# Router logits of a retention-and-experts kernel: row-block sums kept in PSUM on two column quarters, and one weight piece loaded earlier

## The chip, the cores and the metric

One core of one Trainium2 chip runs the whole program. The metric is the device time of one execution in microseconds, measured over several runs. TensorE (PE in the views, its weight loads PEld) does matrix products from SBUF into PSUM, VectorE (DVE) and ScalarE (ACT) do elementwise work, GpSimd (POOL) does elementwise work and indirect DMAs, and SyncE (SP) issues most plain DMAs, one after the other in program order.

## The reference, cut to what matters

```python
# q, k, v: (4, 8, 768, 64); x = retention(q, k, v) as (3072, 512); 8 experts, F = 1024
xn = x / (np.linalg.norm(x, axis=-1, keepdims=True) + 1e-06)
en = expert_emb / (np.linalg.norm(expert_emb, axis=-1, keepdims=True) + 1e-06)
logits = xn @ en.T / tau
expert_idx = np.argmax(logits, axis=1)
...
gate_w = probs[np.arange(N), expert_idx]      # probs = softmax(logits)
for e in range(E):
    mask = expert_idx == e
    h = np.maximum(x[mask] @ w1[e], 0.0)
    out[mask] = gate_w[mask, None] * (h @ w2[e])
```

## The kernel before, in words

The program has two halves. The first is the retention: 12 steps `m` of the loop over `NM`, each 256 tokens with all 8 heads. A step computes scores (L398), masks them on VectorE (L419), adds the products with the running state (`inter`, L466) and with the values (`intra`, L466), updates the state (`state`, L433), and turns the next step's keys (L367) and queries (L385). ScalarE copies the result into `yTs[m]`, a tile with the 512 features on partitions in `KT` = 4 row blocks of 128 and the 256 tokens along the free axis.

The router works on a step's result one step later. `logits_products` multiplies each of the 4 row blocks of `yTs[m]` (128 features x 256 tokens, fp32) with the scaled expert embedding `enT[:, j]` (128 features x 32 columns, 8 of them real). Row block j writes its own quarter of the PSUM bank's partitions (32j to 32j+31), so the four products go to four column quarters of the array, and none of them adds to another. `logits_rows` transposes the bank in 32x32 blocks on VectorE into `parts` (L523). A token's logits are then still in four parts, on four groups of 32 partitions. `sums` (L533) adds them at the end of each group of steps (`GROUPS`): four small TensorE products with a 0/1 matrix, one for each quarter of the tokens, into a free corner of a PSUM bank. `choose` (L547 to L556) takes the maximum and the first expert that reaches it, `add_counts`, `count` and `ranks` turn that into a slot number, and `place` writes the token's row to the table `tbl` by an indirect DMA from GpSimd. At step 3 the logits of steps 0, 1 and 2 are made in one go.

The second half is the experts. The 64 weight pieces (512 KB each, tile `raw`) come through `load_piece` in 4 buffers; ScalarE and VectorE split each into a high and a low part (`whi` L239, `wlo` L243), and TensorE runs three products for each weight block (L265 first layer, L1117 and L1163 second layer). The first expert starts early: as soon as the first token blocks are placed, `early_slots` reads their table rows (L637), `early_gather` fetches the tokens (`xge`, L628), TensorE turns them (L647), and `products` fills TensorE while VectorE and GpSimd finish the routing of the last steps. SyncE's order there is `early_slots(0)`, the rows of step 8 to memory (`rows`, L502), `early_slots(1)`, `early_slots(2)`, then, behind the last early gather (`gathered`), the first expert's fourth piece (four DMAs, L211), two pieces of its second layer (L220), and the rows of steps 9 and 10. `rows_turn(11)` (L495) reuses the buffer that the rows of step 9 are written from.

Tiles `hh`, `hl` (hidden layer) and `xh`, `xl` (tokens) are laid out with a row pitch taken from `PITCH[e]`.

The order on every engine is the order in which the program is written, since the kernel schedules by hand.

Of the kernel before, what the change touches and what calls it, by code (L numbers as in the profile page):

```python
# [11 lines left out]
F32 = mybir.dt.float32  # L12
F32R = mybir.dt.float32r
# [28 lines left out]
CAP = max(CAPS)  # L42
NXC = -(-CAP // Q)
CAPW = NXC * Q
PITCH = [CAP if c % P == 0 else c if e == NE - 2 else CAPW for e, c in enumerate(CAPS)]
OV = 352
EARLY = 280
TURNED = [c % P > 0 and e < NE - 1 for e, c in enumerate(CAPS)]
# [61 lines left out]
def retention_moe(ctx: ExitStack, tc: tile.TileContext, q, k, v, emb, tau, w1, w2, const, const16, out):  # L110
# [10 lines left out]
    def C(name):  # L121
        lo, hi = _AT[name]
        return cst1[:, lo:hi] if hi <= _C1 else cst2[:, lo - _C1:hi - _C1]
# [255 lines left out]
    def transpose_q(m, s, copy=nc.scalar.copy):  # L379

        if m not in qTs:
            qTs[m] = ap_.tile([P, NQ, 2, KT, Q], F32, name="qT")
        ps = pt_()
        for g in range(NQ):
            nc.tensor.transpose(ps[:, g * P:(g + 1) * P], qs_r[:, m % 3, 4 * s + g], ident)  # L385
        return copy(out=qTs[m].rearrange("p g u j (t s) -> p (g u) j t s", s=2)[..., s],
                    in_=ps.rearrange("p (g t j) -> p g j t", g=2 * NQ, j=KT))
# [124 lines left out]
    def logits_products(m, ps=None):  # L512
        ps = pt_() if ps is None else ps
        for j in range(KT):
            nc.tensor.matmul(ps[j * Q:(j + 1) * Q, :T2], enT[:, j, :], yTs[m][:, j, :], start=True, stop=True,  # L515
                             skip_group_check=True)
        return ps

    def logits_rows(m, ps):
        g = group_of[m]  # L520
        if g not in parts:
            parts[g] = ap_.tile([P, max(map(len, GROUPS)), 2, NQ, Q], F32, name="parts")
        nc.vector.transpose(out=parts[g][:, m - GROUPS[g][0]].rearrange("p u g e -> p (u g) e"),  # L523
                            in_=ps[:, :T2].rearrange("p (g b) -> p g b", b=Q))

    def span(g):
        return slice(2 * GROUPS[g][0], 2 * GROUPS[g][-1] + 2)
# [1 line left out]
    def sums(g, ps=None, fresh=False, room=None):  # L529
        nm = len(GROUPS[g])  # L530
        ps = pt_() if ps is None else ps
        for i in range(NQ):
            nc.tensor.matmul(ps[i * Q:(i + 1) * Q, :2 * nm * NE], C("quarters"),  # L533
                             parts[g][:, :nm, :, i, :NE].rearrange("p m u e -> p (m u) e"), start=not fresh, stop=True,
                             skip_group_check=True)
        at = room if fresh else ps[:, 64:]
        return [a[:, :2 * nm * NE].rearrange("p (n e) -> p n e", e=NE) for a in (ps, at)] + [at[:, 48:48 + NE]]

    chosen = []

    def choose(g, zs):
        z, w, _ = zs
        r = span(g)
        nb = r.stop - r.start
        bc = lambda t: t.unsqueeze(2).broadcast_to([P, nb, NE])
        m = ap_.tile([P, nb], F32, name="m", bufs=1)
        nc.vector.tensor_reduce(out=m, in_=z, axis=AX.X, op=ALU.max)  # L547
        yield
        nc.vector.tensor_tensor(out=z, in0=z, in1=bc(m), op=ALU.subtract)
        yield  # L550
        nc.vector.scalar_tensor_tensor(out=w, in0=z, scalar=0.0,
                                       in1=C("e16").unsqueeze(1).broadcast_to([P, nb, NE]), op0=ALU.is_lt, op1=ALU.add)
        yield
        nc.vector.tensor_reduce(out=wmn[:, r], in_=w, axis=AX.X, op=ALU.min)
        yield
        chosen.append(nc.vector.tensor_tensor(out=oh[:, r], in0=w, in1=bc(wmn[:, r]), op=ALU.is_equal))  # L556
        yield
# [77 lines left out]
    def early_slots(j):  # L635
        n = EROWS[j][1]
        sealed.append(nc.sync.dma_start(out=tb[:n, 0, j], in_=tbl[j * P:j * P + n, :2 + NE]))  # L637
# [173 lines left out]
    for m in range(NM):  # L811
# [12 lines left out]
                i = o[0]  # L824
        n = 2 if m < 7 else 3 if m < 9 else 4
        if m == NM - 2:
            early_slots(1)
            held, ready = ready, []
        if m == 0:
# [21 lines left out]
        if m == 0:  # L851
            state(0)
            state_copy(0)
            state_sums(0)
            next(emb_steps)
            intra(0, 0)
            intra(0, 1)
            transpose_k(1, 0)
            i = transpose_k(1, 1)
            after(load_v(2), i)  # L860
            inter(0)
            transpose_q(1, 0)
            i = transpose_q(1, 1)
            for j in (*load_q(3), load_k(3), load_v(3)):
                after(j, i)
            state(1)
            state_copy(1)
            state_sums(1)
        else:
            inter(m)  # L870
            if nxt:
                i = state(m + 1)
                if 6 < m < NM - 3:
                    for x, (f, s) in enumerate(scales):
                        after(f(m + 2, s), first)
                        if x < n:
                            place_one(i)
                if m == NM - 3:
                    after(scale_k(m + 2, 0), spread)
                    for _ in range(3):  # L880
                        place_one(i)
                    scale_k(m + 2, 1)
                    scale_q(m + 2, 0)
                    place_one(i)
                if m == NM - 2:
                    place(held)
                    after(placed[-len(held)], i)
                    early_slots(2)
                    early_gather(0)
                    early_gather(1)  # L890
                    gathered = early_gather(2)
                    for j, n in EROWS:
                        tokens(n, 0, slice(j, j + 1))
                    load_piece(gathered)
                state_copy(m + 1)
                if m + 3 < NM:
                    after(load_k(m + 3), i)
            if m == 2:
                after(nc.sync.dma_start(
                    out=tbl.rearrange("(e s) c -> e (s c)", e=NE)[:, :FILL * SW].rearrange("e (p x) -> e p x", p=P // NE),  # L900
                    in_=none), i)
            for i in () if m < 3 else (0, 1, 2) if m == 3 else (m - 1,):
                logits_rows(i, logits_products(i))
            if m == NM - 5:
                pad(0, spare(0, 3), True)
            if m == NM - 3:
                pad(1, spare(1, 3, 2 * NE), True)
            if m == NM - 2:
                pad(2, bank("pst1"))
            if nxt:  # L910
                state_sums(m + 1)
                if m == NM - 2:
                    lows[0]()
                transpose_k(m + 1, 0)
                transpose_q(m + 1, 0)
                i = transpose_q(m + 1, 1)
                if m + 3 < NM:
                    after(load_v(m + 3), i)
                transpose_k(m + 1, 1)
                if done is not None:  # L920
                    z = sums(done, spare(0, done % 3), True, spare(0, 3))
                    run_all(choose(done, z))
                    run_all(add_counts(done, z))
                if m == NM - 2:
                    lows[1]()
                if m == NM - 2:
                    load_piece(gathered)
                    load_piece(gathered)
                rows(m - 1, gathered if m == NM - 2 else None)
                intra(m, 0)  # L930
                intra(m, 1)
            else:
                intra(m, 0)
                take(m, 0)
                rows_turn(m - 1, (0,))
                z = sums(done)
                run_all(choose(done, z))
                run_all(add_counts(done, z))
                rows_turn(m - 1, (1,))
                rows(m - 1, x=xs_[m - 1])  # L940
                intra(m, 1)
# [146 lines left out]

    xts = {}

    def columns(name, k, e):
        t = hp.tile([P, k, CAPW], F32R, name=name)
        return t.rearrange("p k c -> p (k c)")[:, :k * PITCH[e]].rearrange("p (k c) -> p k c", k=k)

    def x_turn(e, kt):
        if kt == 0:
            xTs[e] = (columns("xh", KT, e), columns("xl", KT, e))
        xt = xts[e, kt] = mp.tile([P, NXC, Q], F32, name="xt", bufs=2)
        n = blocks_of(e)
        nc.vector.transpose(out=xt[:, :n], in_=xgs[e][:, :n, kt * Q:(kt + 1) * Q])  # L1100
        nc.scalar.copy(out=xTs[e][0][:, kt, :CAPS[e]], in_=xt.rearrange("p n b -> p (n b)")[:, :CAPS[e]])
# [175 lines left out]
    for e in range(1, NE):  # L1277
        nxt = e + 1 < NE
        c = CAPS[e]
        cols = slice(0, c)  # L1280
        hh, hl = columns("hh", FT, e), columns("hl", FT, e)
        gsteps = iter(())
        last = None
        for ft in range(FT):
# [166 lines left out]
```

## Time and profile before

| what | value |
|---|---|
| median of 3 runs | 396.85 us (396.44 to 399.21) |
| the profiled execution | 396.12 us |
| its span on the engines | 394.3 us |
| TensorE matmul busy | 384.3 us, 97% of the span |
| VectorE, ScalarE, GpSimd busy | 252.6, 214.6, 154.8 us |
| granted TensorE clock | 1.0 |

The profiled execution is 0.73 us below the median. The span begins with the first instruction; the rest of the execution's time lies around it. Two of the three runs lie close together and the third is 2.4 us above them.

### The profile page before, as it was taken

The page shows a single profiled execution, that of the slowest core. Times are in us where ns is not written, and L with a number is a line of the kernel's source. Part 1 is how long each engine was busy: PE and PEld are TensorE (multiplying, and loading weights), DVE is VectorE, ACT ScalarE, POOL GpSimd, SP SyncE. Part 2 cuts the span into 40 slices and gives each one's busy share as a digit, 9 for nine tenths or more (in the row PEclk, how much of TensorE's full clock was granted, in tenths as well). Part 3 has the DMA queues.
Part 4 walks back from the last instruction along what each step waited for, and adds up shares of the span by engine and source line. Part 5 has one row for each costly group of instructions (what it writes and reads, how often), then busy time and mean ns, then how long its engine had stood idle before and what let it go on. Part 6 is the DMA issues. An engine that isn't in the chain of part 4 may idle for free.

```text
span 394.3 us, 9699 instructions
## 1 busy us (share of the span) xinstructions
PE 384.3 (97%) x3714; PEld 359.4 (91%) x3714; DVE 252.6 (64%) x536; ACT 214.6 (54%) x383; POOL 154.8 (39%) x177
## 2 busy tenths in 40 slices
PE   7999999988999999999999999999999999999995
PEld 3899888877879898999999999999889999999985
DVE  5496876977988648853871874667357756476500
ACT  3585566655876175526553843935675534573411
POOL 2856397585844614203802510530282131121032
PEclk9999999999999999999999999999999999999999
DMA  7898999689469787976778796886979676675121
GB/s 237 260 305 256 268 267 281 180 240 262 98 197 288 237 249 217 298 183 225 251 244 215 257 333 184 256 282 204 264 259 347 191 230 227 169 240 158 30 107 56
DMA packets 91029, 89.20 MB, mean 226 GB/s; under 512 B 10796, under 2 KB 69548, under 8 KB 90972
## 3 DMA queue, kind: packets, MB, share of 16 engines
q1 hardware_dynamic: 85916, 75.39, 64.1%
q0 software_dynamic: 4880, 13.03, 9.2%
q8 instruction: 31, 0.51, 0.6%
q14 instruction: 26, 0.21, 0.2%
q10 hardware_dynamic: 176, 0.07, 0.1%
HBM read 65.00 MB, written 18.79 MB: 212 GB/s over the span
## 4 chain that ended last, share of the span: by engine, by line
PE 77%; DMA 13%; DVE 4%; issue 2%; SPq 1%; POOL 1%; POOLq 0%; ACT 0%; DVEq 0%
DMA out_dram<-og,si 10%; PE b L265 10%; PE pst L1117 9%; PE py L466 9%; PE py L265 8%; PE py L1117 7%; PE pst L265 6%; PE b L398 6%; PE b L1117 4%; PE pst L433 3%; PE pst L1163 3%; PE b L367 3%; PE b L385 2%; PE b L515 2%; PE pst L1203 2%
## 5 line engine op out<-in xcount | busy, mean ns | idle before, releaser
L243 DVE TENSOR_TENSOR wlo<-raw,whi 128x1024 fp32r<-128x1024 f32 x64 | 77.6, 1217 | 15.9 <-ACT whi L239 12.9
L1144 POOL DMA_INDIRECT out_dram<-og,si x26 | 27.0, 1039 | 115.0 <-ACT og L1134 65.2
L239 ACT CAST whi<-raw 128x1024 fp32r<-128x1024 f32 x64 | 66.1, 1044 | 1.3 <-DMA raw<-in_moe_w_dram 1.2
L628 POOL DMA_INDIRECT xr<-xd,gi x24 | 29.3, 1220 | 29.5 <-ACT sq L297 14.9
L265 PE MATMUL b<-xh,whi 128*128 128x360 f32 (+5 forms) x104 | 34.3, 334 | 0.0
L265 PE MATMUL b<-xl,whi 128*128 128x360 f32 (+5 forms) x104 | 34.1, 332 | 0.0
L265 PE MATMUL b<-xh,wlo 128*128 128x360 f32 (+5 forms) x104 | 34.0, 332 | 0.0
L419 DVE TENSOR_TENSOR pm<-b,mask 128x512 f32<-128x512 f32 x48 | 29.8, 683 | 4.8 <-PE b L398 4.5
L1100 DVE STREAM_TRANSPOSE xt<-xg 128x384 f32<-128x384 f32 (+1 forms) x28 | 15.6, 578 | 25.4 <-DMA xg<-xs 25.3
L270 ACT ACTIVATE hh<-b 128x360 fp32r<-128x360 f32 (+5 forms) x26 | 12.6, 484 | 34.9 <-PE b L265 34.9
L356 POOL TENSOR_TENSOR hh<-whi,cst 128x512 f32<-128x512 f32 x22 | 23.1, 1068 | 19.5 <-DVE pm L419 14.3
L599 POOL DMA_INDIRECT tbl<-zt,sloti x24 | 25.4, 1060 | 12.6 <-DVE sloti L590 3.5
L1117 PE MATMUL pst<-hh,wlo 128*128 128x360 f32 (+4 forms) x88 | 29.4, 334 | 0.8 <-DVE wlo L243 0.8
L1117 PE MATMUL pst<-hl,whi 128*128 128x360 f32 (+4 forms) x88 | 29.4, 334 | 0.0
L1117 PE MATMUL pst<-hh,whi 128*128 128x360 f32 (+4 forms) x88 | 29.3, 332 | 0.0
L265 PE MATMUL py<-xl,whi 128*128 128x384 f32 (+5 forms) x84 | 27.7, 334 | 0.0
L265 PE MATMUL py<-xh,whi 128*128 128x384 f32 (+5 forms) x84 | 27.5, 333 | 0.0
L265 PE MATMUL py<-xh,wlo 128*128 128x384 f32 (+5 forms) x84 | 27.2, 330 | 0.0
L361 POOL TENSOR_TENSOR hl<-wlo,cst 128x512 f32<-128x512 f32 x22 | 22.8, 1052 | 10.0 <-DMA wlo<-in_k_dram 8.3
L466 PE MATMUL py<-pm,vs 128*64 128x128 f32 x384 | 24.4, 277 | 1.0 <-issue 1.0
L398 PE MATMUL b<-qT,kT 64*128 64x128 f32 x384 | 24.7, 278 | 0.0
L466 PEld LDWEIGHTS py<-pm,vs 128*64 128x64 f32 x384 | 21.0, 137 | 3.0 <-issue 1.7
(237 smaller groups left out, 1026.0 us busy)
## 6 DMA issues: line engine op xcount, KB each, us to landing
raw<-in_moe_w_dram SPq DMA_DIRECT2D x60, 512.0 KB, 4.7
whi<-in_q_dram SPq DMA_DIRECT2D x24, 256.0 KB, 4.0
xd<-x SPq DMA_DIRECT2D x48, 128.0 KB, 6.3
wlo<-in_k_dram SPq DMA_DIRECT2D x11, 512.0 KB, 6.1
xs<-xr SPq DMA_DIRECT2D x6, 768.0 KB
og<-yt SPq DMA_DIRECT2D x72, 48.0 KB, 3.1
whi<-in_v_dram SPq DMA_DIRECT2D x6, 512.0 KB
wlo<-in_v_dram SPq DMA_DIRECT2D x6, 512.0 KB
```

The lines of the kernel that those rows point to most:

```text
L239: nc.scalar.copy(out=views[1], in_=views[0])
L243: nc.vector.tensor_tensor(out=views[2], in0=views[0], in1=views[1].bitcast(F32), op=ALU.subtract)
L265: nc.tensor.matmul(acc[:, :w], a, x[:, kt, cols], start=(n == 0), stop=(n == len(todo) - 1))
L356: return eng.tensor_tensor(out=qs_r[:, m % 3, :, a], in0=qin[m % 3][:, a], in1=w, op=ALU.mult)
L361: return eng.tensor_tensor(out=ks_r[:, m % 3, s, h], in0=kin[m % 3][:, h, s], in1=w[:, h], op=ALU.mult)
L398: nc.tensor.matmul(psc[a][:, j], kTs[m][a * D:(a + 1) * D, j, u].rearrange("p s c -> p (s c)"), q_cols(m, a, j, u), start=True, stop=True, ...
L419: o.append(nc.vector.tensor_tensor(out=pm, in0=psc[a], in1=w, op=ALU.mult))
L466: nc.tensor.matmul(pys[m][u][o * D:(o + 1) * D, j], lhsT, rhs, start=first, stop=True, skip_group_check=True)
L599: i = nc.gpsimd.indirect_dma_start(out=tbl[:, :], out_offset=bass.IndirectOffsetOnAxis(ap=sloti[:, n:n + 1], axis=0), in_=zt[:, n], in_off ...
L628: return nc.gpsimd.indirect_dma_start(out=xr[:n, j, :], out_offset=None, in_=xd[:rows_, :], in_offset=bass.IndirectOffsetOnAxis(ap=gi[:n, ...
L1117: nc.tensor.matmul(acc[:, :c], a[:, f], x[:, kt, :c], start=(n == 0), stop=(n == 3 * FT - 1))
L1144: i = nc.gpsimd.indirect_dma_start(out=out[:, :] if h is None else out.rearrange("t (h x) -> (t h) x", h=2), out_offset=bass.IndirectOffse ...
```

## The change

Five edits:

1. `logits_products` makes 8 products of 128 columns in place of 4 of 256. The tokens of a step are taken in two sets of columns (`i` = 0, 1), each set goes to one quarter of the partitions (0 to 31, 32 to 63), and the four row blocks add up there in PSUM.
2. `logits_rows` then transposes 64 partitions x 64 twice in place of 128 x 256, straight into the complete logits, and the four products of `sums` are gone. `choose` reads the logits from `parts` in SBUF and keeps the maximum in PSUM.
3. At step 3 the logits of steps 1 and 2 move between the turns of the next step's keys and queries.
4. The fourth raw piece is loaded on SyncE ahead of `early_slots(1)` and waits for no gather.
5. `hh` and `hl` have the pitch `CAPW` = 416 for all experts, and the tokens of expert 6 have it too (360 before).

```diff
-PITCH = [CAP if c % P == 0 else c if e == NE - 2 else CAPW for e, c in enumerate(CAPS)]
+PITCH = [CAP if c % P == 0 else CAPW for c in CAPS]
...
         for j in range(KT):
-            nc.tensor.matmul(ps[j * Q:(j + 1) * Q, :T2], enT[:, j, :], yTs[m][:, j, :], start=True, stop=True,
-                             skip_group_check=True)
+            y = yTs[m][:, j].rearrange("p (u g b) -> p g u b", u=2, b=Q)
+            for i in range(2):
+                nc.tensor.matmul(ps[i * Q:(i + 1) * Q, :P].rearrange("p (h u b) -> p h u b", h=2, b=Q), enT[:, j, :], y[:, i::2],
+                                 start=(j == 0), stop=(j == KT - 1), skip_group_check=True)
...
-        nc.vector.transpose(out=parts[g][:, m - GROUPS[g][0]].rearrange("p u g e -> p (u g) e"),
-                            in_=ps[:, :T2].rearrange("p (g b) -> p g b", b=Q))
+        for h in range(2):
+            nc.vector.transpose(out=parts[g][2 * h * Q:2 * (h + 1) * Q, m - GROUPS[g][0]],
+                                in_=ps[:2 * Q, 2 * h * Q:2 * (h + 1) * Q].rearrange("p (u b) -> p u b", b=Q))
...
-        for i in range(NQ):
-            nc.tensor.matmul(ps[i * Q:(i + 1) * Q, :2 * nm * NE], C("quarters"),
-                             parts[g][:, :nm, :, i, :NE].rearrange("p m u e -> p (m u) e"), start=not fresh, stop=True,
-                             skip_group_check=True)
...
-        nc.vector.tensor_reduce(out=m, in_=z, axis=AX.X, op=ALU.max)
+        s = parts[g][:, :nb // 2, :, :NE].rearrange("p m u e -> p (m u) e")
+        nc.vector.tensor_reduce(out=m, in_=s, axis=AX.X, op=ALU.max)
...
         if m == NM - 2:
+            load_piece()
             early_slots(1)
...
                         tokens(n, 0, slice(j, j + 1))
-                    load_piece(gathered)
...
-            for i in () if m < 3 else (0, 1, 2) if m == 3 else (m - 1,):
+            if m > 2:
+                i = 0 if m == 3 else m - 1
                 logits_rows(i, logits_products(i))
...
+                if m == 3:
+                    logits_rows(1, logits_products(1))
                 i = transpose_q(m + 1, 1)
...
                 transpose_k(m + 1, 1)
+                if m == 3:
+                    logits_rows(2, logits_products(2))
...
-        hh, hl = columns("hh", FT, e), columns("hl", FT, e)
+        hh = hp.tile([P, FT, CAPW], F32R, name="hh")
+        hl = hp.tile([P, FT, CAPW], F32R, name="hl")
```

TensorE's order at step 3, from the first logits product to the values' products of `intra`, before:

```order
L515 MATMUL b_777<-yT,enT 32x256 x4
L515 MATMUL b_784<-yT,enT 32x256 x4
L515 MATMUL b_790<-yT,enT 32x256 x4
L367 MATMUL b_800<-ident,hl 128x128 x4
L385 MATMUL b_808<-ident,hh 128x128 x4
L385 MATMUL b_814<-ident,hh 128x128 x4
L367 MATMUL b_821<-ident,hl 128x128 x4
L533 MATMUL pst_591<-parts,cst_61 32x48 x4
L466 MATMUL py_698<-pm_710,vs 64x128
```

The same place after the change:

```order
L517 MATMUL b_777<-yT,enT 32x128 x8
L367 MATMUL b_793<-ident,hl 128x128 x4
L385 MATMUL b_801<-ident,hh 128x128 x4
L517 MATMUL b_807<-yT,enT 32x128 x8
L385 MATMUL b_818<-ident,hh 128x128 x4
L367 MATMUL b_825<-ident,hl 128x128 x4
L517 MATMUL b_831<-yT,enT 32x128 x8
L466 MATMUL py_698<-pm_710,vs 64x128
```

Here 24 logits products of 128 columns stand where 12 of 256 stood, in three places instead of one, and the sums product of the group (L533) is gone; the order around it is unchanged.

SyncE's order from the loads of the first three pieces to the rows of steps 9 and 10 (`tb` is the table read of `early_slots`, `xd` the rows in memory), as one piece of the difference:

```order
 L211 DMA raw<-in_moe_w_dram 32x2x512 x4
-L637 DMA tb<-tbl 128x10
-L502 DMA xd<-x 256x1x128 x4
-L637 DMA tb<-tbl 128x10
-L637 DMA tb<-tbl 24x10
+L636 DMA tb<-tbl 128x10
+L502 DMA xd<-x 256x1x128 x4
 L211 DMA raw<-in_moe_w_dram 32x2x512 x4
+L636 DMA tb<-tbl 128x10
+L636 DMA tb<-tbl 24x10
 L220 DMA raw<-in_moe_w_dram 128x2x512 x2
 L502 DMA xd<-x 256x1x128 x8
```

The second L211 row, the fourth piece, stood behind all three table reads and now stands ahead of the second and the third.

## Rows read from the trace of the kernel before

**Rows 1.** The page, part 1: busy time, share of the span, instructions.

```profile
PE 384.3 (97%) x3714; PEld 359.4 (91%) x3714; DVE 252.6 (64%) x536; ACT 214.6 (54%) x383; POOL 154.8 (39%) x177
```

**Rows 2.** Waits of TensorE, whole span: total us, times, longest us.

```profile
PE pst L433 <- issue: 1.2, 1, 1.2
PE py L466 <- issue: 1.0, 1, 1.0
PE pst L1117 <- DVE wlo L243: 0.8, 2, 0.4
```

**Rows 3.** Chain that ended last, by time: start us, us, what.

```profile
38.71 1.43 PE b L515 x24
40.14 0.59 PE b L367 x4
...
41.60 0.44 PE b L367 x4
42.04 0.22 PE pst L533 x8
...
48.36 0.57 PE b L515 x8
...
50.83 1.90 PE py L466 x32
```

**Rows 4.** Timeline of TensorE, step 11: start us, us, what.

```profile
110.08 1.09 PE L466 MATMUL py<-pm,vs 128*64 128x128 f32 x16
111.10 0.27 PE L533 MATMUL b<-parts,cst 128*32 128x32 f32 x8
111.30 1.09 PE L466 MATMUL py<-pm,vs 128*64 128x128 f32 x16
```

**Rows 5.** Chain by time, first layers of experts 5 and 6.

```profile
293.07 3.97 PE b L265 x24
...
324.60 3.94 PE b L265 x24
```

**Rows 6.** Timeline of SyncE's issues, 97 to 122 us.

```profile
99.03 3.50 SPq L502 DMA_DIRECT2D xd<-x  x4
...
103.60 2.67 SPq L637 DMA_DIRECT2D tb<-tbl  x2
...
112.01 1.76 SPq L211 DMA_DIRECT2D raw<-in_moe_w_dram  x4
...
114.86 6.02 SPq L502 DMA_DIRECT2D xd<-x  x8
```

**Rows 7.** Timelines of GpSimd and TensorE around the early gathers.

```profile
107.28 0.21 POOL L622 TENSOR_SCALAR gi<-tb 128x1 int32<-128x1 f32 x1
...
112.33 0.87 PE L647 MATMUL pst<-ident,xge 128*128 128x128 f32 x6
```

**Rows 8.** Timelines of VectorE and TensorE, 116 to 133 us.

```profile
116.66 0.17 DVE L547 TENSOR_REDUCE m<-b 128x2 f32<-128x16 f32 x1 [0.69 <-PE b L533]
...
122.36 1.31 DVE L495 STREAM_TRANSPOSE x<-yT 128x512 f32<-128x512 f32 x2 [0.91 <-DMA xd<-x]
...
130.61 0.40 PE L1117 MATMUL pst<-hh,wlo 128*128 128x280 f32 x1 [0.35 <-DVE wlo L243]
...
132.10 0.40 PE L1117 MATMUL pst<-hh,wlo 128*128 128x280 f32 x1 [0.45 <-DVE wlo L243]
```

**Rows 9.** Timeline of TensorE: its two stops that no engine ends.

```profile
86.78 1.20 PE L466 MATMUL py<-pm,vs 128*64 128x128 f32 x17 [1.00 <-issue]
...
93.17 0.34 PE L433 MATMUL pst<-whi,hl 64*64 64x64 f32 x7 [1.16 <-issue]
```

**Rows 10.** Windows: length, busy (x) of PE, PEld, DVE, ACT, POOL, PEclk, DMA, GB/s.

```profile
78.50:82.30 3.80, 3.80 (x134) 3.50 (x130) 3.25 (x6) 2.23 (x5) 3.11 (x4) 1.00 0.82 234
86.50:93.10 6.60, 5.23 (x127) 4.78 (x127) 5.09 (x11) 2.98 (x5) 3.35 (x4) 1.00 0.91 258
```

**Rows 11.** The page, part 3: DMA queue of instructions: packets, MB, share.

```profile
q8 instruction: 31, 0.51, 0.6%
```

More of the change, by code (lines that the diff above doesn't have):

```diff
@@ L521, in logits_rows @@
         if g not in parts:
-            parts[g] = ap_.tile([P, max(map(len, GROUPS)), 2, NQ, Q], F32, name="parts")
-        nc.vector.transpose(out=parts[g][:, m - GROUPS[g][0]].rearrange("p u g e -> p (u g) e"),
-                            in_=ps[:, :T2].rearrange("p (g b) -> p g b", b=Q))
+            parts[g] = ap_.tile([P, max(map(len, GROUPS)), 2, Q], F32, name="parts")
+        for h in range(2):
+            nc.vector.transpose(out=parts[g][2 * h * Q:2 * (h + 1) * Q, m - GROUPS[g][0]],
+                                in_=ps[:2 * Q, 2 * h * Q:2 * (h + 1) * Q].rearrange("p (u b) -> p u b", b=Q))
     def span(g):
@@ L531, in sums @@
         ps = pt_() if ps is None else ps
-        for i in range(NQ):
-            nc.tensor.matmul(ps[i * Q:(i + 1) * Q, :2 * nm * NE], C("quarters"),
-                             parts[g][:, :nm, :, i, :NE].rearrange("p m u e -> p (m u) e"), start=not fresh, stop=True,
-                             skip_group_check=True)
         at = room if fresh else ps[:, 64:]
-        return [a[:, :2 * nm * NE].rearrange("p (n e) -> p n e", e=NE) for a in (ps, at)] + [at[:, 48:48 + NE]]
+        return [a[:, :2 * nm * NE].rearrange("p (n e) -> p n e", e=NE) for a in (ps, at)] + [at[:, 48:48 + NE], at[:, 56:56 + 2 * nm]]
     chosen = []
     def choose(g, zs):
-        z, w, _ = zs
+        z, w, _, m = zs
         r = span(g)
@@ L545, in choose @@
         bc = lambda t: t.unsqueeze(2).broadcast_to([P, nb, NE])
-        m = ap_.tile([P, nb], F32, name="m", bufs=1)
-        nc.vector.tensor_reduce(out=m, in_=z, axis=AX.X, op=ALU.max)
+        s = parts[g][:, :nb // 2, :, :NE].rearrange("p m u e -> p (m u) e")
+        nc.vector.tensor_reduce(out=m, in_=s, axis=AX.X, op=ALU.max)
         yield
-        nc.vector.tensor_tensor(out=z, in0=z, in1=bc(m), op=ALU.subtract)
+        nc.vector.tensor_tensor(out=z, in0=s, in1=bc(m), op=ALU.subtract)
         yield
@@ L1089, in retention_moe, with columns @@
     xts = {}
-    def columns(name, k, e):
-        t = hp.tile([P, k, CAPW], F32R, name=name)
-        return t.rearrange("p k c -> p (k c)")[:, :k * PITCH[e]].rearrange("p (k c) -> p k c", k=k)
+    def columns(name, e):
+        t = hp.tile([P, KT, CAPW], F32R, name=name)
+        return t.rearrange("p k c -> p (k c)")[:, :KT * PITCH[e]].rearrange("p (k c) -> p k c", k=KT)
     def x_turn(e, kt):
         if kt == 0:
-            xTs[e] = (columns("xh", KT, e), columns("xl", KT, e))
+            xTs[e] = (columns("xh", e), columns("xl", e))
         xt = xts[e, kt] = mp.tile([P, NXC, Q], F32, name="xt", bufs=2)
```

## Prediction

> **What bounds the kernel now.** I began with the page: TensorE is busy for 97% of the span, the next engine (VectorE) for 64% [rows 1]. The waits of TensorE then say what the other 3% are: inside the program there are only two stops of 1.2 and 1.0 us that no engine ends, and 0.8 us before the first expert's second layer [rows 2]; the rest is the start and the last outputs. So TensorE's own work sets the time nearly everywhere, and a microsecond added to its stream is a microsecond of the kernel, unless it falls into one of those waits. The chain of waits, read by time, gives the price of each kind of block, since there one TensorE block ends where the next begins [rows 3]. Last I read the timelines of the four other engines at the seam between retention and experts [rows 6 to 8], where the chain leaves TensorE.
>
> **Products of the logits.** Each fp32 product stands in the trace as two matmul rows, so the "x8" of one step counts 4 weight loads and matmuls twice over. Before, one step's logits (4 products of 256 columns, on four column quarters) take 0.57 us from their start to the next block [rows 3]. That is short because the four run side by side. After, there are 8 products of 128 columns on two quarters: the same number of columns in all, but only two abreast, and each row block must follow the one before it on its quarter. The trace has a block of nearly this shape: `intra` of one half step is 8 products of 128 columns with 128 rows of weights, two abreast on two column halves, and takes 1.02 us, from 110.08 to 111.10 [rows 4]. The weights are 64 columns wide there and 32 here, which can only make their load shorter; the lead-in before the second pair and the drain behind the last are in the 1.02. Without lead-in and drain it is 0.88, what a second such half adds where both stand in one piece (1.90 less 1.02) [rows 3, 4], the lower bound; the upper bound is no overlap of the two quarters, a rival below. I take 1.02, the row of the same shape: +0.45 for each block that stands alone. There are nine (steps 4 to 11, and the last step's block at the seam): +4.05 us.
>
> At step 3 the three blocks ran in one piece of 1.43 us [rows 3]. Now each is alone, and the second one cuts the turns of the queries in two: the turn behind a logits block takes 0.59 us where one behind another turn takes 0.44 [rows 3], so one more change of that kind costs 0.15. 3 x 1.02 + 0.15 - 1.43 = +1.78 us. Spreading them gains nothing back, since TensorE has no wait at step 3 that this could fill [rows 2].
>
> **The sums.** Six sums blocks vanish from TensorE, each some 0.2 us (0.22 at step 3; 0.20 at step 11, from 111.10 to 111.30) [rows 3, 4]: -1.2 us. All six stand in TensorE's stream, so all of it counts. On VectorE, the transposes read a quarter of the elements, in two instructions, and `choose` needs no TensorE product first. VectorE waits for TensorE in the loop, so what it saves there only makes that wait longer, and I cost it at nothing; the work that hides it is TensorE's own stream, and without that cover the saving would still not be a loss. The new waits in the order (VectorE on its own transposes, TensorE's turns on logits products that ended two blocks earlier) are for things long done.
>
> **The weight piece.** Its four issues take 1.76 us on SyncE [rows 6]. Before, they came behind the last early gather, at 112.01, and held up what follows: two second-layer pieces and the rows of step 9, which began at 114.86. Without them these rows begin about 1.8 us earlier and have 0.5 MB less ahead of them. Their landing is what VectorE waits 0.91 us for before it may write the last step's rows at 122.36, and from there VectorE works almost without a gap to the weight parts that TensorE waits for, 0.35 us at 130.61 and 0.45 us at 132.10 [rows 8]. VectorE also no longer waits 0.69 us for the last sums, but that is given back at once in a wait for TensorE's counts, since that comes at a fixed place of its stream. With the 0.91 gone both waits close but for a remainder: -0.7 us (bounds 0 and -0.8). What is next late is nothing: behind it TensorE runs its products unbroken.
>
> On the other side the piece now stands ahead of the table reads of the second and third early slots, on the same queue. SyncE is free from 102.5 (99.03 plus 3.50) until the second read's issue at 103.60 [rows 6], so 1.76 us of issues push that read by at most 0.7. GpSimd uses it at 107.28 [rows 7]. TensorE turns the gathered tokens at 112.33 without a wait [rows 7]; between the held placements and that point TensorE gets two longer logits blocks and loses one sums block, +0.7 us, which covers the delay. I take 0; the price without that cover is a rival.
>
> **The pitch.** The experts' first layers read tokens at a pitch of 416 (expert 5) and 360 (expert 6) at the same rate, 3.97 and 3.94 us for 24 products [rows 5]. So 0, with a few tenths either way.
>
> **The two stops.** They are 254 matmul and load rows apart (127 and 127) [rows 9, 10], and the instruction queue moved 31 packets for TensorE's 7428 rows, some 240 each [rows 1, 11]. I read them as an instruction packet that came late, while the DMA engines were 91% busy [rows 10]. The change adds 16 rows for each logits block and takes 16 for each sums block, 80 by step 7, so the borders of the packets fall elsewhere: 80 rows ahead, and the 254 rows in front of the border are then about those of the window from 78.50 to 82.30, where 264 rows run in 3.8 us, against 5.2 us busy for the 254 between the stops [rows 10]. Denser rows leave less time for the packet, so I expect one longer stop in place of two: +0.3, with bounds of -2.2 (both gone) and +2.5 (6.3 us between the borders less 3.8).
>
> **The sum.** 4.05 + 1.78 - 1.2 - 0.7 + 0.3 = +4.2 us. On the profiled execution's 396.12 that is 400.3; it lay 0.73 below the median, so on the median it is 401.0, 1.06% slower. A measurement of this kernel tells about 1% from no change (the three runs span 0.7%), so the bound of slower is 400.8: my forecast stands just beyond it.
>
> **Rivals.**
>
> *Both stops vanish.* Place: TensorE's stream at steps 7 and 8. If the shifted borders fall where the packet comes in time, 2.2 us return, and the +0.3 is not paid: 401.0 - 2.5 = 398.5, not slower. It decides from the point where a packet lands before 254 rows have run, 3.8 us in the dense window. For it: elsewhere in the retention no packet was late. Against it: the DMA is 82% busy in that window too [rows 10].
>
> *The gather comes late.* The table read queues behind 0.5 MB of weights as well as behind their issues. Were its landing 2.5 us later, GpSimd's three gathers would shift and TensorE would wait at the turn of the gathered tokens; less the 0.7 of cover, +1.5: 402.5. Against it: from 104 us on nothing else is on that queue [rows 6].
>
> *The two quarters don't overlap.* If the passes of the two quarters ran one after the other, each block would pay the 0.88 of its eight pairs twice, twelve times: 401.0 + 12 x 0.88 = 411.6. The row against it is `intra`, which has the same full height of 128 weight rows and runs two abreast [rows 4].
> [...]
>
> *The change does less than it says.* If the wider pitch or the lighter VectorE sped up the experts, the sum could end below 393; no row shows a wait there that this would shorten.
>
> **How the numbers follow.** The forecast 0.58 (0.41 of it beyond 400.8, 0.17 within 1%), both stops gone 0.24 (within 1%, 0.01 of it faster), a late gather 0.10, no overlap 0.04, an unseen gain 0.04. That gives slower 0.55, within 1% 0.40, faster 0.05. The range runs from both stops gone, 398.4, to the longer stop's bound and part of a late gather, 404.0; no overlap and the unseen gain are left out.
>
> **What would show it.** Right: a step's logits block of 1.0 us on TensorE where 0.57 stood, no sums block, the rows of step 9 issued right behind two second-layer pieces, and no wait for `wlo` at the seam. Wrong: a logits block under 0.8 us or over 1.2, a wait of the turns for the gathered tokens, stops without a releaser that sum to much less or more than 2.5 us, or TensorE idle at step 3.

## The result, and the profile after

The changed kernel takes 402.35 us (median of 6 runs, 401.19 to 403.49) against 397.59 us for the kernel before in the same comparison: a ratio of 1.0115 with a 95% interval of 1.0088 to 1.0143, so 4.6 us slower. A second comparison, beside runs of before on its own chip (`e11_after_again` below), gave 1.0107 (1.0081 to 1.0133), 4.2 us. The forecast was +4.2 us, 1.06%. Of all executions reported here two, both of `e7_border_shift` (403.21 and 406.89 us), count as slow, and its ratio leaves them out.

The profiled execution of after took 403.2 us, with a span of 401.3 us. That is 7.0 us above the span before, more than the ratio says; what the surplus is shows below, where the second profile is read. The busy time of the engines, first part of the page (answers to [rows 1]):

```profile
PE 390.4 (97%) x3762; PEld 366.4 (91%) x3762; DVE 253.7 (63%) x548; ACT 214.6 (53%) x383; POOL 155.6 (39%) x177
```

TensorE has 6.1 us more to do and still sets the time; VectorE is no lighter (253.7 us, +1.1), though its transposes read a quarter of the elements. What TensorE waits for, after (answers to [rows 2]; columns: us in all, times, longest):

```profile
PE pst L1121 <- DVE wlo L243: 1.3, 2, 0.8
...
PE b L398 <- ACT kT L372: 1.2, 2, 0.8
PE b L265 <- DVE wlo L243: 0.6, 1, 0.6
PE py L466 <- issue: 0.5, 2, 0.2
PE py L466 <- ACT yT L486: 0.5, 1, 0.5
```

The two stops of 1.2 and 1.0 us that no engine ended [rows 2, 9] are gone; the waits for the weight parts at the seam [rows 8] are still there; and there are new waits for ScalarE's copies. The price of a block, from the chain of waits at step 3 and step 4 (columns: start, us, what; answers to [rows 3]):

```profile
38.39 1.00 PE b L517 x16
39.38 0.59 PE b L367 x4
39.97 0.44 PE b L385 x4
40.41 1.00 PE b L517 x16
41.41 0.59 PE b L385 x4
42.00 0.44 PE b L367 x4
42.43 1.00 PE b L517 x16
43.43 1.90 PE py L466 x32
...
49.53 1.00 PE b L517 x16
```

A logits block is 1.00 us where 0.57 stood, at step 4 and at each step behind it (1.02 at step 11), and no sums block (L533) follows it. Step 3 lasts from 38.39 to 43.43, 5.04 us; before it was 38.71 to 42.26 (the end of the sums that began at 42.04), 3.55 us [rows 3].

SyncE's queue around the moved load, after (answers to [rows 6]):

```profile
100.91 3.22 SPq L502 DMA_DIRECT2D xd<-x  x4
104.18 2.01 SPq L211 DMA_DIRECT2D raw<-in_moe_w_dram  x4
106.29 3.51 SPq L636 DMA_DIRECT2D tb<-tbl  x2
114.77 0.91 SPq L220 DMA_DIRECT2D raw<-in_moe_w_dram  x2
115.77 6.16 SPq L502 DMA_DIRECT2D xd<-x  x8
```

The load's four issues (2.01 us) stand ahead of the two table reads, as the edit says. The rows of step 9 come right behind the two second-layer pieces, but at 115.77 and not 1.8 us earlier than the 114.86 of before, since those pieces stand behind the gathers, and GpSimd issued the last of them at 112.17 instead of 109.47.

### The profile page after: what moved, and what is told of

The parts are those of the page before. It is cut to its first block, busy times and chain, and to the rows that moved or that the text cites. A ratio compares the mean times of both kernels' runs of the same rounds, so it can differ in the third digit from the quotient of the medians.

```text
span 401.3 us, 9813 instructions
## 1 busy us (share of the span) xinstructions
PE 390.4 (97%) x3762; PEld 366.4 (91%) x3762; DVE 253.7 (63%) x548; ACT 214.6 (53%) x383; POOL 155.6 (39%) x177
## 4 chain that ended last, share of the span: by engine, by line
PE 66%; DMA 14%; SPq 6%; DVE 5%; issue 4%; ACT 2%; POOL 1%; POOLq 0%; DVEq 0%; ACTq 0%
DMA out_dram<-og,si 10%; PE py L466 8%; PE b L265 7%; PE py L265 7%; PE pst L1121 6%; PE b L398 6%; PE py L1121 6%; PE pst L265 5%; SPq L1133 4%; PE pst L433 3%; PE b L1121 3%; PE pst L1167 3%; PE b L517 3%; PE b L367 3%; PE b L385 2%
## 5 line engine op out<-in xcount | busy, mean ns | idle before, releaser
L466 PE MATMUL py<-pm,vs 128*64 128x128 f32 x384 | 24.4, 276 | 0.5 <-issue 0.5
L398 PEld LDWEIGHTS b<-qT,kT 64*128 64x128 f32 x384 | 22.4, 188 | 2.5 <-ACT kT L372 1.5
```

Of the source, the lines that this page charges most:

```text
L398: nc.tensor.matmul(psc[a][:, j], kTs[m][a * D:(a + 1) * D, j, u].rearrange("p s c -> p (s c)"), q_cols(m, a, j, u), start=True, stop=True, ...
L466: nc.tensor.matmul(pys[m][u][o * D:(o + 1) * D, j], lhsT, rhs, start=first, stop=True, skip_group_check=True)
```

## The experiments

The kernels of one group ran on one chip, beside the kernel before; its median was 393.87 us in the first group, 396.85 in the second and 396.67 in the third. So ratios are compared, not times.

**First group: the parts.** `e1_logits_only` is before with edits 1 and 2 (new products, transposes into `parts`, no sums) and step 3 left in one piece (the diff is shortened, here and for `e4_four_quarters`).

```diff
-    for j in range(KT):  matmul(ps[j*Q:(j+1)*Q, :T2], enT[:, j, :], yTs[m][:, j, :], start=True, stop=True)
+    for j in range(KT):
+        for i in range(2):  matmul(ps[i*Q:(i+1)*Q, :P], enT[:, j, :], y[:, i::2], start=(j == 0), stop=(j == KT-1))
```

> The kernel before with edits 1 and 2 alone (products on two quarters, sums in PSUM, no sums products), step 3 still in one piece, load and pitch as before. My theory, that TensorE's longer logits blocks are the whole of the loss: 9 single blocks x 0.43, and the piece of step 3 at 2.75 in place of 1.43 (1.00 plus twice 0.88), +1.3, less 1.2 for the sums: +4.0 us (1.0%). Rival, that the loss comes from the moved load or from the split of step 3: within 1 us of before.

Measured: 399.51 us, ratio 1.0144 (1.0098 to 1.0190). The edits of the logits alone give the whole loss; the 1.0% that was expected lies inside the interval.

`e2_load_only` is before with edit 4 alone.

```diff
         if m == NM - 2:
+            load_piece()
             early_slots(1)
...
-                    load_piece(gathered)
```

> The kernel before with edit 4 alone (the fourth piece ahead of the second early slot). The prediction's term: -0.7 us, no wait of TensorE for wlo at the seam. Rival, from the profile after, where these waits still stand: 0 or a loss up to 1 us, with VectorE held by something else than the rows' landing.

Measured: 394.6 us, ratio 1.0010 (0.9980 to 1.0039): no gain is seen, and the -0.7 us of the prediction (0.9982) lies just inside the interval. Its profile shows what took the place of the old waits. TensorE waits for the gathered tokens:

```profile
PE pst L647 <- DMA xge<-xd,gi: 0.9, 1, 0.9
PE b L647 <- DMA xge<-xd,gi: 0.7, 1, 0.7
```

The 0.35 and 0.45 us for `wlo` [rows 8] are gone, as the step on the load forecast. The first of the new waits, 0.85 us at 110.0, is at the early gathers: the rival "the gather comes late" is here too. The second, 0.72 us at 136.36, is at a later gather of the first expert, behind the seam.

`e3_no_load_move` is after without edit 4.

```diff
-            load_piece()
             early_slots(1)
...
+                    load_piece(gathered)
```

> The changed kernel without edit 4. If the moved load gains 0.7, this is 0.7 us slower than the changed kernel, some 5.4 us above before; if it costs, this is faster, 3.5 to 4.5 us above before.

Measured: 399.1 us, ratio 1.0150 (1.0110 to 1.0191). With the load where it was, the loss is the same within the intervals. Whether the moved load gives some tenths back beside the slower blocks (1.0150 here, 1.0115 and 1.0107 for the whole change) is inside them too, and on different chips; it stays open. The profile of this run shows TensorE's stream with almost no waits behind the start, neither stops nor waits for ScalarE, `wlo` or the gathered tokens (both waits of its list):

```profile
PE b L757 <- DVE x L738: 1.3, 1, 1.3
PE b L562 <- DVE zt L577: 0.2, 1, 0.2
```

So it serves below to price the blocks alone.

`e4_four_quarters` is e1 with the tokens in four sets on all four quarters, 16 products of 64 columns for a step, so that no sums are needed and four products run abreast again.

```diff
-            for i in range(2):  ... y[:, i::2]      # 128 columns
+            for i in range(NQ): ... y[:, i]         # 64 columns
```

> Edits 1 and 2 on four quarters: 16 products of 64 columns, four abreast, each token group on its own quarter, the row blocks summed in PSUM, one transpose of 128 x 64, no sums products; the rest as before. If the number abreast is what the change lost, a block takes about 0.6 us (32 rows of 64 columns four abreast take 0.46 in the state update, plus lead-in and drain) and the kernel loses nothing on the blocks and gains the sums: -1.0 us, 0.2 to 0.3% under before. If instead each product has a fixed cost of its own, 16 products cost more than 8: a block over 1 us and some 4 us above before.

Measured: 399.01 us, ratio 1.0117 (1.0079 to 1.0155), a miss. The block costs what was expected; one step of the chain of waits:

```profile
49.97 0.58 PE b L517 x32
```

But TensorE stopped elsewhere. Its waits:

```profile
PE b L517 <- issue: 2.6, 2, 2.0
PE pst L1114 <- DVE wlo L243: 2.2, 3, 0.9
...
PE pst L644 <- DMA xge<-xd,gi: 0.6, 1, 0.6
PE b L367 <- issue: 0.5, 1, 0.5
```

Three stops that no engine ends, 3.1 us in all, ate more than the 1.2 us that the missing sums give, and the waits for `wlo` and for the gathered tokens came on top. Where TensorE ran, the blocks did what was expected: from the first scores (8.66 us) to the first expert's first product (114.92) it took 106.26 us, 102.62 without the three stops and the wait for the tokens, against 103.35 before without its two stops (the ends of this stretch are shown under "How the sum came out"). That asked for the second and third group.

**Second group: the price of a block, and the stops.** `e5_products_twice` is after with each logits product issued twice.

```diff
-        for j in range(KT):
+        for j in [*range(KT), *range(KT)]:
```

> After, with every product of the logits issued twice over (the sum in PSUM is then twice the logits, which changes no index of the largest but the weights of the experts): 16 rows more in each of the 12 blocks. Theory (a block is TensorE's own work in a full stream): each block takes 0.88 us longer, 1.88 instead of 1.00, so 12 x 0.88 = +10.6 us on after's 402.35, 413 us, and 1.0155 x 1.027 = 1.04 against before (two or three tenths of it may be lost in waits that close). Rival (the time of after comes from waits and stops and a block hides beside them): under +5 us, below 407.

Measured: 411.56 us, ratio 1.0349 (1.0302 to 1.0396), 0.0234 above after: 9.3 us. A block in its chain of waits:

```profile
52.88 1.87 PE b L517 x32
```

So eight more products cost 0.87 us, and 12 blocks of that are 10.4 us; what is missing lies within the interval. So a block stands on TensorE's path with nearly its full length.

`e8_one_after_other` is after with all four products of the first quarter ahead of all four of the second.

```diff
-        for j in range(KT):
-            for i in range(2):
+        for i in range(2):
+            for j in range(KT):
```

> After, with the same products of the logits, but all four of the first quarter ahead of all four of the second, so that neighbours share a quarter and only one pair of them can run side by side. Theory (two products on different quarters run side by side, and that is what keeps a block at 1.00 us): a block takes about 1.00 + 6/8 x 0.88 = 1.7 us, so 12 x 0.7 = +8 us on after, 410 us, ratio to before about 1.03. Rival (a weight load waits for the products before it in any order, so that the order of the quarters makes no difference): blocks stay at 1.00 us and the time at after's, ratio 1.011.

Measured: 404.64 us, ratio 1.0188 (1.0140 to 1.0236). A block in its chain:

```profile
51.09 1.46 PE b L517 x16
```

1.46 us where 1.7 was expected and the rival had 1.00: the order counts, so products on different quarters do run side by side. They still do so in part here: in the block at 60.35 the second quarter's first pass starts at 60.81, when the first quarter is only at its fifth of eight. Twelve blocks of 0.46 us more are 5.5 us, but the kernel is only some 3 us slower than after. The profiles differ in waits too: behind the start TensorE waits 1.0 us in all here and 2.6 in `e11_after_again`, so part of the longer blocks may have gone into waits that closed; that is not shown further.

`e7_border_shift` is before with 50 short warm-up products where 10 long ones stood: 80 matmul and load rows more ahead of the first data, and none behind.

```diff
-    for _ in range(W0):      matmul(idle, zeros[:, :P], zeros)
+    for _ in range(5 * W0):  matmul(idle[:Q, :80], zeros[:, :Q], zeros[:, :80])
```

> Before, with 50 short products of zeros ahead of the first block where 10 long ones stood: 80 rows more for TensorE before the program's data has landed, so no work is added to its stream, but every border of TensorE's instruction packets falls 80 rows earlier in the program. Theory (the stops that no engine ends are packets that come late): the two stops of 1.2 and 1.0 us at steps 7 and 8 move or vanish though the work is the same, and the time changes by up to 2.2 us either way. Rival (they belong to the work at that place): the same two stops at the same blocks, and the same time.

Measured: 399.68 us (median of the ten executions that the ratio uses, 396.39 to 401.09), ratio 1.0067 (1.0034 to 1.0099). So another warm-up, done before the data has come, made the same program slower. What slows it is not shown: the profiled execution, 397.18 us, is one of its fastest, and its first expert's first product starts at 114.69 us, as in before. (The warm-up is also shorter, 3.31 us where 4.42 stood; the granted clock is 1.00 from the start in both.) Where the stops fall is told by counting matmuls from the start of the span up to a stop. Busy time by engine from 0 to each of the two stops of before (columns: window, length, then busy us and number of instructions for PE, PEld, DVE, ACT, POOL, then clock, DMA share, GB/s):

```profile
0.00:85.60 85.60, 83.19 (x1620) 71.15 (x1620) 61.49 (x137) 52.36 (x94) 54.17 (x71) 1.00 0.86 255
...
0.00:91.85 91.85, 88.45 (x1747) 75.91 (x1747) 66.98 (x152) 55.34 (x99) 58.39 (x75) 1.00 0.87 257
```

The same of the border shift, up to its one stop without a releaser (0.82 us, inside a logits block):

```profile
0.00:81.65 81.65, 78.83 (x1620) 70.36 (x1620) 60.54 (x130) 50.11 (x90) 50.98 (x68) 1.00 0.89 264
```

And of the four quarters, up to its three stops:

```profile
0.00:38.85 38.85, 37.16 (x729) 30.79 (x730) 25.77 (x52) 23.72 (x42) 22.96 (x41) 1.00 0.90 269
...
0.00:67.25 67.25, 63.54 (x1366) 55.08 (x1367) 44.56 (x96) 39.76 (x71) 39.52 (x57) 1.00 0.88 260
...
0.00:84.50 84.50, 80.27 (x1748) 70.51 (x1749) 58.98 (x130) 50.16 (x90) 51.16 (x68) 1.00 0.88 259
```

The doubled products (`e5_products_twice`) have one such stop, 0.89 us:

```profile
0.00:41.15 41.15, 39.33 (x729) 32.75 (x730) 27.18 (x55) 24.36 (x44) 24.46 (x42) 1.00 0.92 274
```

In before and in the border shift the stop stands behind the 1620th matmul, though that is another instruction of the program; in the four quarters and the doubled products one stands behind the 729th. And 729, 1366, 1620, 1748 lie five, two and one times some 127 matmuls apart (637, 254, 128), 127 being the distance of the two stops of before. Counted exactly, with the semaphore instructions between them, TensorE's instructions up to these seven stops are 1473, 2753, 3265 or 3521, each 193 more than a multiple of 256. So the stops belong to a fixed grid of instructions, not to the work at that place.

The trace also has the packets of the instruction queue, 16,384 bytes each. One lies just ahead of each stop of before (part 3 of the DMA view from 84.4 to 86.8 us; from 90.8 to 93.2 us the line is the same):

```profile
q8 instruction: 1, 0.02, 2.5%
```

They landed at 85.41 and 91.80 us, and TensorE went on at 86.78 and 93.17, 1.37 us later both times. At the other five stops it went on 1.37 to 1.51 us after such a landing. That the stops are late instruction packets, which the prediction had read from one profile, is what these seven stops point to.

`e6_pitch_only` is before with edit 5 alone.

```diff
-PITCH = [CAP if c % P == 0 else c if e == NE - 2 else CAPW for e, c in enumerate(CAPS)]
+PITCH = [CAP if c % P == 0 else CAPW for c in CAPS]
```

> Before, with the change of the pitch alone. Theory: 0 (first-layer blocks of 3.94 to 3.97 us at either pitch), ratio 1.000, within 0.4%. Rival (the wider pitch slows the sixth and seventh expert's products or VectorE's copies): +0.5 us or more behind the fifth expert. As the change touches nothing ahead of the experts, its profile also shows whether the two stops of steps 7 and 8 stand on this chip at the same places in the program.

Measured: 397.06 us, ratio 0.9997 (0.9973 to 1.0022): nothing. Its profile has neither of the two stops of before, though the program is the same up to the experts: whether a packet comes late on this grid differs between executions of the same stream. It has other waits instead, 0.6 and 0.4 us for ScalarE's copies.

**Third group: after again, and the borders in it.** `e11_after_again` is the changed kernel, unchanged.

> The changed kernel itself once more, as the unshifted partner of the border shift. Theory: ratio 1.0115 within 0.4%; a second profile shows logits blocks of 1.00 us again. The waits of TensorE for ScalarE at steps 9 and 10 and for the weight parts at the seam, which were some 2.8 us in the first profile of it, are either there again (then they belong to the change) or differ by over 1 us (then they belong to the execution).

Measured: 400.77 us (400.49 to 401.78), ratio 1.0107 (1.0081 to 1.0133); span of the profiled execution 398.6, 4.3 us above before. TensorE's timeline at the places that matter (columns: start, us, what; in brackets the idle time and what ended it):

```profile
65.42 0.76 PE L466 MATMUL py<-qT,s 64*64 64x128 f32 x10 [0.57 <-ACT yT L486]
...
100.00 2.06 PE L398 MATMUL b<-qT,kT 64*128 64x128 f32 x32 [0.40 <-ACT kT L372]
...
114.79 0.44 PE L646 MATMUL pst<-ident,xge 128*128 128x128 f32 x2
116.01 0.66 PE L646 MATMUL pst<-ident,xge 128*128 128x128 f32 x4 [0.78 <-DMA xge<-xd,gi]
...
118.45 0.76 PE L265 MATMUL py<-xh,whi 128*128 128x280 f32 x4
```

The waits for ScalarE are there again, 1.0 us in place of 1.7, and those for `wlo` are not. Neither kind belongs to the change: `e6_pitch_only`, with the old blocks, waits 1.0 us for ScalarE, and `e3_no_load_move`, with the new ones, not at all. The wait for the gathered tokens is new against the first profile. SyncE and GpSimd ahead of it:

```profile
103.64 2.03 SPq L211 DMA_DIRECT2D raw<-in_moe_w_dram  x4
105.77 4.14 SPq L636 DMA_DIRECT2D tb<-tbl  x2
...
112.16 0.21 POOL L621 TENSOR_SCALAR gi<-tb 24x1 int32<-24x1 f32 x1 [0.72 <-DMA tb<-tbl]
```

The table reads begin at 105.77 and the last of them ends the wait of GpSimd at 112.16; before they began at 103.60 and GpSimd had its last index at 108.95 without a wait for them:

```profile
108.95 0.21 POOL L622 TENSOR_SCALAR gi<-tb 24x1 int32<-24x1 f32 x1
```

`e9_after_border` is after with the border shift of e7.

> After, with the 50 short products of zeros of the border shift in place of the 10 long ones: 80 rows more ahead of the first block, no work added to the stream. Theory (the place of the packet borders is worth up to 3 us, and it is part of after's time): the ratio to before differs from that of the unshifted after, run on the same chip, by 0.3% or more in either direction (the shifted kernel before was 0.67% slower), and stops stand at other blocks. Rival (borders are of no account in after): the same ratio within 0.25%, near 1.0115.

Measured: 400.13 us, ratio 1.0090 (1.0058 to 1.0122), against 1.0107 for the unshifted kernel beside it: 0.17% apart, the rival's side. Neither profile of after nor this one has a stop without a releaser above 0.4 us in the retention, so there was nothing to move.

`e10_four_border` is the four quarters with the border shift.

> The logits on all four quarters (blocks of 0.58 us, no sums), with the border shift. Theory (its blocks are worth -1.2 us, and what ate that were three stops of 3.1 us at the sixth, eleventh and fourteenth packet border, and what they made late): with the borders 80 rows earlier in the program the stops move; if they vanish the time is 0.3% below before, if others come it stays up to 1.2% above. Rival (the smaller products themselves cost time): 1.012 as before, with blocks above 0.58 us or the same stops at the same blocks.

Measured: 401.72 us, ratio 1.0123 (1.0089 to 1.0157), as without the shift. The blocks are 0.58 us, and the three stops without a releaser are gone; waits for other engines came. The longest is 2.9 us at step 9, where TensorE, VectorE and ScalarE stand still together. VectorE and ScalarE there:

```profile
96.16 0.25 DVE L525 STREAM_TRANSPOSE parts<-b 128x64 f32<-128x64 f32 x1 [3.41 <-remote]
...
96.31 0.59 ACT L372 COPY kT<-b 128x512 f32<-128x512 f32 x1 [4.40 <-remote]
```

Both needed TensorE blocks that by their rows ended by 92.1 and 92.6 us (ends of matmuls are modelled in the trace), and they went on at 96.16 and 96.31 us. What held them 3 to 4 us, the trace doesn't tell ("remote"). An instruction packet landed at 94.95 us, 1.2 us ahead of that, but the stop is not on the grid (4040 instructions, 200 more than a multiple of 256), so the cause stays open.

## Why the prediction was right, step by step

**The products of the logits: right, and the main cause.** The forecast was +0.45 for each single block, from `intra`'s 1.02 [rows 4]; the block is 1.00, so nine of them cost 3.9 and not 4.05 us. The load rows are the shorter ones, as the step said: 110 ns for the 32 columns of L517 after, 137 for the 64 of `intra`'s L466 before (medians). Three runs show that this is TensorE's own time: the same edit alone gives 1.0144 (e1), twice the products give 0.87 us more a block (e5; the prediction's row without lead-in and drain was 0.88), and products in the other order 0.46 us more (e8). It goes with the number of quarters at work: the same 1024 columns a step took 0.57 us on four quarters before, 0.58 on four in e4, 1.00 on two.

**"The two quarters don't overlap" is refuted** by the same rows: that rival had blocks of twice 0.88 us. The load rows of e4, in the answer on its products' line, last as long as those of before's blocks (L515, 106/109/110; ns, min/median/max):

```profile
L517 PEld LDWEIGHTS b<-yT,enT x384: 106/110/110, 38.1 to 114.7; 128*32 128x32 f32 x192
```

Of 32 passes in 0.58 us each quarter has 8, so a pass takes at most 73 ns, less than the 110 of its load row: as this trace records them, the loads did not stand between the products of the same quarter.

**Step 3: right.** +1.78 for the blocks and -0.22 for its sums were forecast, +1.56; the two stretches differ by 5.04 less 3.55, +1.49.

**The sums: right.** No L533 block is left; the other five were some 0.2 us each.

**The two stops: the step that failed, as to sign.** One longer stop was forecast, +0.3; both vanished, -2.2, the rival's way. The reading behind it held: they are late instruction packets on a grid of some 254 rows (e7, e4, e5). What the step had wrong is that denser rows decide: whether a given packet is late could not be foreseen from one profile, since e6, with the same stream up to there, has no stop at these places.

**The moved load: the step that failed, as to what is late next.** -0.7 was forecast: the rows of step 9 land sooner, VectorE's wait of 0.91 us for them closes [rows 8], and with it the waits for `wlo`. The first link held: none of the six profiles with the load moved has this wait, and five of the seven with the load in place have it (0.15 to 1.52 us). The second did not hold. In the first profile of after VectorE does not wait for the rows, but it stands 1.66 us with no releaser ahead of them, and both waits for `wlo` are there:

```profile
123.84 0.45 DVE L271 SCALAR_TENSOR_TENSOR hl<-py,hh 128x280 fp32r<-128x280 f32 x1 [1.66 <-issue]
127.69 1.30 DVE L495 STREAM_TRANSPOSE x<-yT 128x512 f32<-128x512 f32 x2
...
135.93 0.40 PE L1121 MATMUL pst<-hh,wlo 128*128 128x280 f32 x1 [0.81 <-DVE wlo L243]
...
137.42 0.40 PE L1121 MATMUL pst<-hh,wlo 128*128 128x280 f32 x1 [0.45 <-DVE wlo L243]
```

They stand in e9 too (1.1 us), are gone in e2 and e11, and are gone in e3, whose load was not moved. So the load's place alone does not decide them. In e2 and e11 TensorE waits for the tokens of the early gathers instead, 0.85 and 0.78 us. The prediction let the table read slip by at most 0.7 and had +0.7 of TensorE's work to cover it. In e11 the read began 2.2 us later than before, but TensorE came to the turn of the tokens 2.5 us later as well (114.79 and not 112.33); what nothing covered is that the read lasted 4.14 in place of 2.67 us. That the moved load makes it longer is not shown: e4, with the load in place, has 3.64 us and a wait of 0.56, and e8, with the load moved, 4.13 us and no wait.

**How the sum came out all the same.** The stretch from the first scores to the first expert's first product, before and in e3:

```profile
9.18 2.06 PE L398 MATMUL b<-qT,kT 64*128 64x128 f32 x32
...
114.69 0.76 PE L265 MATMUL py<-xh,whi 128*128 128x280 f32 x4
...
8.48 2.06 PE L398 MATMUL b<-qT,kT 64*128 64x128 f32 x32
...
115.92 0.76 PE L265 MATMUL py<-xh,whi 128*128 128x280 f32 x4
```

Before it is 105.51 us, 103.35 without the two stops; in e3, which has neither stops nor the other waits, it is 107.44 (the two executions are of different groups). So the blocks and the missing sums cost 4.1 us up to there, where the prediction's terms give 4.05 + 1.78 - 1.0 = 4.8; 0.25 of the difference stands under the blocks and step 3 above, the rest is open. In after the waits come on top. Up to that product (114.69 us before, 118.45 in e11, +3.76) the pieces are: start -0.62 (first scores at 8.56 us and not 9.18, by the first data), step 3 +1.49, nine blocks +3.9, four more sums -0.8 (the last stood behind this point), stops -2.2; that is +1.8, and the remaining 2.0 are about the three waits shown for e11, each with the gap that it makes: 0.73 at 64.69, 0.45 at 99.55, 1.0 at 115.0. So the blocks were as forecast, and two misses of opposite sign, stops that went (2.5 us better) and waits that came (some 2 to 3 us worse), cancelled. That the total fell on the forecast is partly luck. The first profile's surplus of 2.7 us over e11 is more of such waits: for ScalarE at steps 9 and 10, for `wlo` at the seam and again at 198.76 us (0.63), inside the experts. What makes TensorE and ScalarE wait for each other there was not shown; e10's rows have a longer stop of that kind, 3 to 4 us.

**The pitch: right**, 0.9997 alone (e6).

## What to carry to other kernels

Cost a block on column quarters by how many of them it keeps busy, and take the price from a row of the same shape: half the quarters at the same number of columns doubled what a further block of the same products adds, from 0.43 us (half of 1.43 less 0.57 at step 3, before) to 0.87 (e5), and saving a small second product (0.2 us) did not pay for it. In a stream that is busy for 97%, small stalls replace one another: an edit that closes one wait (the weight parts) or moves one stop is worth only what the next late thing leaves of it (in e2 0.8 us of waits for `wlo` went and 1.6 for the gathered tokens came), so ask for that one, and take a second profile before a stall of a microsecond is put down to the change. More and shorter matmuls can cost more than their own time: with 480 rows more, both runs on four quarters lost what the missing sums gave and 1.2% besides, e4 in good part at three late instruction packets (3.1 us), e10 at waits whose cause stays open.

## What the runs showed of the hardware that was not expected

- The stops that no engine ends stand on a grid of some 127 matmuls with their loads, counted from the start of the program (193 more than a multiple of 256 instructions, seven stops in four programs), and each ends 1.37 to 1.51 us after a packet of the instruction queue has landed. 80 rows of warm-up ahead of the data moved one to other work; that kernel was 0.67% slower (0.34 to 0.99), though not by the one stop in its profile, and the same shift gave nothing measurable in after (1.0090 beside 1.0107).
- VectorE's transposes of a quarter of the elements, 64x64 twice, take 0.50 us together (after, L526; 0.24 each) against 0.44 for 128x256 once (before, L523), and 128x64 takes 0.25 (L525, in e10's rows above). So here one instruction with an eighth or a quarter of the elements took more than half the time.
- VectorE and ScalarE went on 3 to 4 us after the recorded end of the TensorE blocks that they waited for, at step 9 of the retention (e10). The cause stays open.
